# Reordering the start, the prologue and the paired output loop of a fused linear-attention and MLP kernel (forward and all gradients, one core)

## The chip, the core and the metric

The kernel runs on one core of a Trainium2 chip. The metric is the device time of one execution in microseconds (us). A profile is one execution taken by the hardware profiler; its "span" runs from the first to the last instruction and is 1.7 to 1.8 us shorter than the device time of the same execution.

Engines are named as in the profile: PE is TensorE's matmuls, PEld its weight loads, DVE is VectorE, ACT is ScalarE, POOL is GpSimd, and SP is the engine whose queue issues most of the DMAs here. "Releaser" means the last event that an instruction waited for.

## The reference

The inputs have a sequence of S = 2048 rows and width D = 640. The function is a gated mix of a linear attention and a ReLU MLP with F = 1728 hidden columns. The task is its output and the gradients with respect to six inputs.

```python
def _A_ref(x, wqkv, wo):                      # H = 32 heads of 20 columns
    q, k, v = split(x @ wqkv)
    phi = lambda t: jnp.where(t > 0, t + 1, jnp.exp(t)) + 1e-6
    pq, pk = phi(q), phi(k)
    kv = einsum("bhsd,bhse->bhde", pk, v)
    z  = einsum("bhsd->bhd", pk)
    o  = einsum("bhqd,bhde->bhqe", pq, kv) / (einsum("bhqd,bhd->bhq", pq, z)[..., None] + 1e-6)
    return o.reshape(B, S, D) @ wo
def _B_ref(x, w1, w2):
    return jnp.maximum(x @ w1, 0) @ w2
# ... shortened: the reshapes into heads and the types are left out
g = sigmoid((x * gate_w).sum(-1, keepdims=True))
out = g * _A_ref(x, wqkv, wo) + (1 - g) * _B_ref(x, w1, w2)
# outputs: out, and the gradients of A_x, A_wqkv, A_wo, B_w1, B_w2, gate_w for a given grad_out
```

## The kernel before

The sequence is cut into 16 chunks of 128 rows. The change touches the first third of the kernel, which goes like this on PE:

1. Start: some warm-up matmuls on a zeroed buffer, transposes of the first x chunks on PE (`xt`), and the k products (`k_chunk`), whose weights carry `gate_w` as a 641st column.
2. `yp`: five tiles of Y = pk' x. Each is transposed by a DMA on its way to `Y_s`.
3. Prologue ("the middle" below): h of chunks 0 and 1, a block-diagonal product `bd`, five tiles of `M`, each again transposed by a DMA, q and h of chunk 2.
4. Main loop: for each chunk, a q product, two halves of h (each 10 matmuls), and an output product `out_chunk`, which needs h of the chunk, and pq of the chunk, both transposed by DMAs.

h has 13.5 blocks of 128 columns. The last half block of two neighbouring chunks is handled by a **tail pair**: one chunk's half uses rows 0 to 63 of the array, the other's rows 64 to 127. So the tail pair of chunk i (even) needs the transposed h of chunk i **and** of chunk i+1.

All DMA transposes are issued from SP's queue, in its program order. This is the code that matters (cuts are marked):

```python
# helpers: L325 is the matmul in mm_cols (most products have this line)
def load_T(dst, src):
    return nc.sync.dma_start_transpose(dst, src.rearrange("s (c p) -> s c p", p=P))

# ---- start
x_load(0, 1)
nc.scalar.dma_start(wk_s[:, 0:2, 0:D], ...)           # two loads of wk
nc.scalar.dma_start(wk_s[:, 2:5, 0:D], ...)
nc.scalar.dma_start(wk_s[:, :, D:D + 1], gate_w.rearrange("(k p o) -> p k o", p=P, o=1))
x_load(1, 2)
x_load(2, G)
# ... cut
for n in range(9):
    nc.tensor.matmul(wp_[:, 0, :], lhsT=warm[:, 0:P], rhs=warm, start=True, stop=True)
# ... cut
xt(0)
xt(1)
for i in range(NT):
    if i + 2 < XPE * G:
        xt(i + 2)
    k_chunk(i)

# ---- q_post ends with   load_T(pqTs[i], pg)   once POOL has made pg
# ---- h_half(i, 1) ends with   load_T(hTs[i], hs(i))
def tail_pair(psA, psB, lA, lB, rhs, last):
    for b, (a, e) in enumerate(DSPL):
        nc.tensor.matmul(psA[:, b, 0:e - a], lhsT=lA[0:FT], rhs=rhs[0:FT, a:e], ...)    # L500
        nc.tensor.matmul(psB[:, b, 0:e - a], lhsT=lB[FT:P], rhs=rhs[FT:P, a:e], ...)    # L501

# ---- middle
h_half(0, 0)
# ... cut: zp, zb
q_den(0)
q_den(1)
h_half(0, 1)
blockdiag(KVT_s, wv_s, Y_s)
q_post(0)
h_half(1, 0)
for t in range(KD):
    mp = pp("mtp")
    win_mms(mp, lambda j: wo_s[:, j, csl(t)], KVT_s)
    copy_out(t, MT_s[:, t, :], flat(mp)[:, 0:D])
    load_T(M_s[:, :, csl(t)], MT_s[:, t, :])
q_post(1)
h_half(1, 1)
# ... cut: three DMAs
do_load(0)
# ---- main loop
LAG = 2
for i in range(2, NT + LAG):
    if i < NT and i % G == 1:
        do_load(i // G)
    if i < NT:
        q_main(i)
        q_den(i)
        h_half(i, 0)
        q_post(i)
        if i % 2 == 0 or i == NT - 1:
            h_half(i, 1)
    if i % 2 == 0 and i <= NT:
        q_store(i // 2 - 1)
    if i >= LAG:
        out_chunk(i - LAG)
    if i < NT - 1 and i % 2 == 1:
        h_half(i, 1)
# ---- loads of the next stage
for g in range(NG):
    load_T(doTg[g], do2[g * G * P:(g + 1) * G * P, :])
    if g < NSP:
        load_N(pqgg[g], pqg_d[g * G * P:(g + 1) * G * P, :])
```

## Time and profile before

| | before |
|---|---|
| device time, median of 4 runs | 646.46 us (645.88 to 647.41) |
| profiled execution | 646.82 us, span 645.0 us |
| PE busy | 636.6 us, 99% of the span |
| idle PE time between its first and last matmul | 4.2 us, of which 3.9 us in four gaps |
| from PE's last matmul to the end | 2.9 us |

The first two parts of the profile page that matter are the busy times (time, share of the span, instructions) and the engines' shares of the chain that ended last:

```profile
PE 636.6 (99%) x4458; PEld 355.3 (55%) x4458; DVE 240.3 (37%) x491; ACT 152.6 (24%) x224; POOL 97.8 (15%) x97
...
PE 94%; DMA 3%; ACT 1%; DVE 1%; issue 0%; POOL 0%; ACTq 0%; SPq 0%; DVEq 0%
```

PE works nearly all the time, so only idle PE time is to be had. The waits of PE name it (engine, product, line, releaser: total us, times, longest us):

```profile
PE op L501 <- DMA arena<-arena: 1.6, 2, 0.9
PE warm L385 <- DVE arena L372: 1.3, 1, 1.3
PE xtp L401 <- DMA arena<-in_A_x_dram: 1.2, 1, 1.2
PE bd L358 <- DMA arena<-arena: 1.1, 1, 1.1
```

The first entry is two tail pairs waiting for a transposed h. The timeline of PE shows where the waits are (start us, duration us, engine, line, operation, idle time before it in brackets). First the start:

```profile
5.07 1.27 PE L401 MATMUL xtp<-ident,arena 128*128 128x128 bf16 x10
7.56 0.45 PE L401 MATMUL xtp<-ident,arena 128*128 128x128 bf16 x5 [1.22 <-DMA arena<-in_A_x_dram]
7.85 1.69 PE L325 MATMUL kp<-arena 128*128 128x512 bf16 x10
```

The first k product begins at 7.85, after a third x chunk has been waited for. Then the middle and the first tail pair:

```profile
59.04 1.12 PE L358 MATMUL bd<-arena 128*128 128x140 bf16 x15
61.27 0.77 PE L358 MATMUL bd<-arena 128*128 128x140 bf16 x10 [1.11 <-DMA arena<-arena]
...
72.72 5.05 PE L325 MATMUL op<-arena 128*128 128x512 bf16 x36
77.71 0.39 PE L500 MATMUL op<-arena 64*128 64x512 bf16 x1
79.02 0.39 PE L501 MATMUL op<-arena 64*128 64x512 bf16 x1 [0.92 <-DMA arena<-arena]
...
79.39 0.93 PE L325 MATMUL qp<-arena 128*128 128x512 bf16 x5
```

`bd` stops after 15 matmuls for Y's last transposed tile. At 77.71 one half of the tail pair runs, and its partner only when the transposed h(1) has landed. The next product starts 1.69 us after the pair began.

### The profile page before, as it was taken

Reading aid. Unit: us, or ns where it says so; the run is one execution under the profiler, and the core shown is the slowest. Engines: PE = TensorE matmul, PEld = TensorE weight load, DVE = VectorE, ACT = ScalarE, POOL = GpSimd, SP = SyncE. Lnnn points to the kernel's source line nnn. Section 1 sums busy time; section 2 is a strip of 40 time slices with the busy share of each in tenths; the row PEclk is TensorE's granted clock in tenths of the full one; section 3 lists DMA queues with packets and bytes.
Section 4 is the critical chain, followed back from the end, with each engine's and each line's share of the span. In section 5 each row is a group of like instructions: output and inputs, shape, how many; then the busy total and the mean of one; then the engine's idle time right before and its main releaser. Section 6 shows DMA issues by size and latency. Waiting matters only on the chain.

```text
span 645.0 us, 10527 instructions
## 1 busy us (share of the span) xinstructions
PE 636.6 (99%) x4458; PEld 355.3 (55%) x4458; DVE 240.3 (37%) x491; ACT 152.6 (24%) x224; POOL 97.8 (15%) x97
## 2 busy tenths in 40 slices
PE   8999999999999999999999999999999999999998
PEld 4555555555555555555555555555555555555554
DVE  3823554454545135655145322130016320104442
ACT  3612222221222123232144343441100111110000
POOL 5002533434334013232001000000000000000000
PEclk9999999999999999999999999999999999999999
DMA  8999964253547953952979997692227549991111
GB/s 207 372 361 243 212 171 116 66 140 95 103 91 126 233 145 104 184 149 83 190 159 216 266 247 142 155 296 64 81 80 163 137 134 251 244 250 42 42 42 42
DMA packets 228409, 103.85 MB, mean 161 GB/s; under 512 B 185098, under 2 KB 227658, under 8 KB 228362
## 3 DMA queue, kind: packets, MB, share of 16 engines
q1 hardware_dynamic: 217050, 90.07, 59.4%
q10 hardware_dynamic: 11312, 13.11, 6.0%
q8 instruction: 35, 0.57, 0.4%
q14 instruction: 12, 0.10, 0.0%
HBM read 28.43 MB, written 28.84 MB: 89 GB/s over the span
## 4 chain that ended last, share of the span: by engine, by line
PE 94%; DMA 3%; ACT 1%; DVE 1%; issue 0%; POOL 0%; ACTq 0%; SPq 0%; DVEq 0%
PE op L325 11%; PE dxp L325 9%; PE gp L701 9%; PE w1p L787 9%; PE w2p L325 9%; PE dp L325 9%; PE hp L487 8%; PE qp L325 3%; PE kp L325 3%; PE yp L325 3%; PE rp L325 3%; PE wkp L325 3%; PE dkp L325 3%; PE xp L685 3%; PE wqp L874 3%; DMA arena<-arena 2%
## 5 line engine op out<-in xcount | busy, mean ns | idle before, releaser
L325 PEld LDWEIGHTS <-arena 128*128 128x128 bf16 x2818 | 218.0, 98 | 169.1 <-issue 2.4
L325 PE MATMUL op<-arena 128*128 128x512 bf16 x576 | 80.7, 299 | 0.0
L487 PE MATMUL hp<-arena 128*128 128x432 bf16 x320 | 62.3, 346 | 0.0
L325 PE MATMUL dxp<-arena 128*128 128x512 bf16 x450 | 61.5, 299 | 0.0
L701 PE MATMUL gp<-arena 128*128 128x432 bf16 x320 | 60.9, 346 | 0.1
L787 PE MATMUL w1p<-arena 128*128 128x432 bf16 x320 | 60.1, 346 | 0.0
L325 PE MATMUL dp<-arena 128*128 128x512 bf16 (+1 forms) x416 | 59.6, 299 | 0.0
L325 PE MATMUL w2p<-arena 128*128 128x512 bf16 (+1 forms) x416 | 59.3, 299 | 0.0
L787 PEld LDWEIGHTS <-arena 128*128 128x128 bf16 x320 | 30.8, 98 | 26.9 <-issue 0.5
L701 PEld LDWEIGHTS <-arena 128*128 128x128 bf16 x320 | 30.5, 98 | 27.0 <-issue 1.7
L487 PEld LDWEIGHTS <-arena 128*128 128x128 bf16 x320 | 30.3, 98 | 25.6
L708 DVE TENSOR_TENSOR arena<-tb,tb 128x864 bf16<-128x864 bf16 x32 | 19.4, 607 | 66.1 <-ACT tb L705 66.0
L456 POOL TENSOR_TENSOR f<-tb,zb 128x640 f32<-128x640 bf16 x16 | 23.3, 1459 | 111.4 <-DVE tb L369 57.8
L705 ACT ACTIVATE tb<-gp,omg_t 128x864 bf16<-128x864 f32 x32 | 31.4, 980 | 31.7 <-PE gp L701 28.4
L771 DVE TENSOR_TENSOR tb<-dkp,dzb 128x640 bf16<-128x640 f32 x16 | 13.1, 819 | 62.5 <-PE dkp L325 62.5
L522 DVE SCALAR_TENSOR_TENSOR tb<-op,arena 128x640 bf16<-128x640 f32 x16 | 13.2, 824 | 48.0 <-ACT arena L520 48.0
L520 ACT CAST arena<-op 128x640 bf16<-128x640 f32 x16 | 11.1, 692 | 83.1 <-PE op L500 43.5
L605 POOL TENSOR_TENSOR f<-zb,grd 128x640 f32<-128x640 bf16 x16 | 20.3, 1268 | 60.2 <-DVE grd L603 60.2
L896 DVE TENSOR_TENSOR arena<-dxp,f 128x640 bf16<-128x640 f32 x15 | 12.3, 823 | 37.0 <-PE dxp L325 37.0
L790 ACT CAST arena<-w1p 128x864 bf16<-128x864 f32 x10 | 8.8, 878 | 72.5 <-PE w1p L787 72.5
L325 PE MATMUL rp<-arena 128*128 128x512 bf16 (+1 forms) x160 | 24.3, 299 | 0.0
L325 PE MATMUL qp<-arena 128*128 128x512 bf16 (+1 forms) x160 | 24.2, 299 | 0.0
(125 smaller groups left out, 624.1 us busy)
## 6 DMA issues: line engine op xcount, KB each, us to landing
arena<-in_A_x_dram SPq DMA_DIRECT2D x7, 640.0 KB, 6.6
out_dram<-arena ACTq DMA_DIRECT2D x28, 160.0 KB, 3.2
pk_d<-arena SPq DMA_DIRECT2D x4, 640.0 KB, 9.3
arena<-in_grad_out_dram SPq DMA_DIRECT2D x4, 640.0 KB, 5.9
e_d<-arena SPq DMA_DIRECT2D x8, 320.0 KB, 3.6
out_dram<-arena ACTq DMA_DIRECT2D x8, 320.0 KB, 2.7
arena<-e_d SPq DMA_DIRECT2D x8, 320.0 KB, 3.5
dq_d<-arena SPq DMA_DIRECT2D x8, 320.0 KB, 4.0
```

What stands on the lines that cost most here:

```text
L325: mm = nc.tensor.matmul(ps_tile[:, b, 0:e - a], lhsT=lhsT, rhs=rhs_fn(a, e), start=start, stop=stop, **kw)
L456: nc.gpsimd.tensor_tensor(tzs[i][:], pqs[i][:], zb[:], ALU.mult)
L487: nc.tensor.matmul(hp[:, nb, 0:NBW], lhsT=xT(i, k), rhs=w1_s[:, k, blk * NBW:(blk + 1) * NBW], start=(k == 0), stop=(k == KD - 1))
L522: nc.vector.scalar_tensor_tensor(jk[:], flat(op)[:, 0:D], 1.0, doX(i)[:, 0:D], ALU.mult, ALU.mult, accum_out=T_t[:, i:i + 1])
L605: nc.gpsimd.tensor_tensor(heads(wz[:]), heads(zb[:]), hb(w32[:]), ALU.mult)
L685: nc.tensor.matmul(xp[:, 0, :], lhsT=lhsT, rhs=doX(i)[:, 0:512], start=(i == 0), stop=(i == NT - 1))
L701: nc.tensor.matmul(gp[:, nb, 0:NBW], lhsT=doTg[i // G][:, k, gsl(i)], rhs=w2T_s[:, k, blk * NBW:(blk + 1) * NBW], start=(k == 0), stop=(k ...
L705: nc.scalar.activation(gs[:], gp[:, :, 0:NBW], ACT.Copy, scale=omg_t[:, i:i + 1])
L708: nc.vector.tensor_tensor(hs(i)[:, rng], msk[:], gs[:].rearrange("p b c -> p (b c)"), ALU.mult)
L771: nc.vector.tensor_tensor(a_[:], flat(kp)[:, 0:D], dzb[:], ALU.add)
L787: nc.tensor.matmul(wp[:, nb, 0:NBW], lhsT=xN2[:, i, csl(m)], rhs=hs(i)[:, blk * NBW:(blk + 1) * NBW], start=(i == 0), stop=(i == NT - 1))
L874: nc.tensor.matmul(wp[:, 0, :], lhsT=lhsT, rhs=dqN[:, i, 0:512], start=(i == 0), stop=(i == NT - 1))
```

## The change

The intent is to remove each of these waits by order alone:

- **Start.** wk comes in five loads; `gate_w` comes as five contiguous rows and is transposed on PE; only x chunk 0 is transposed before the first k product; 8 warm-ups instead of 9.
- **Middle.** Both halves of h(1) are moved forward, one ahead of `bd` and one ahead of the M tiles; q(2) and half of h(2) go between and into the M tiles. M's five DMA transposes become one of 25 blocks, behind all five tiles (`M_s` gets another layout for it).
- **Main loop.** Chunks are handled in pairs: q(a), h(a), q(a+1) and the first half of h(a+1) come ahead of out(a-2).
- **End of the loop.** The loads of grad_out and pq for the next stage are ordered behind the last transpose of h (`after`).

The diff, cut to its core:

```diff
+    M_s = aview("M", KD * D).rearrange("p (t c s) -> p t c s", t=KD, c=KD)
+    def after(late, early):        # order of two DMAs on their queue, no semaphore
+        tc.add_manual_dep(late.ins, early.ins.name, ...)
...
+    wk_load(nc.scalar, 0)
     x_load(0, 1)
-    nc.scalar.dma_start(wk_s[:, 0:2, 0:D], ...)
-    nc.scalar.dma_start(wk_s[:, 2:5, 0:D], ...)
-    nc.scalar.dma_start(wk_s[:, :, D:D + 1], gate_w.rearrange("(k p o) -> p k o", p=P, o=1))
+    wk_load(nc.scalar, 1)
+    wk_load(nc.sync, 2)
+    wk_load(nc.scalar, 3)
+    wk_load(nc.sync, 4)
+    nc.scalar.dma_start(gst[:], gate_w.rearrange("(k p) -> k p", p=P))
...
-    for n in range(9):
+    for n in range(NWARM):          # 8
...
     xt(0)
-    xt(1)
+    nc.tensor.transpose(tp[:, 0, 0:KD], gst[:], ident[0:KD, 0:KD])
+    nc.scalar.copy(wk_s[:, :, D:D + 1], tp[:, 0, 0:KD].unsqueeze(2))
     for i in range(NT):
+        k_chunk(i)
+        if i == 0:
+            xt(1)
         if i + 2 < XPE * G:
             xt(i + 2)
-        k_chunk(i)
...
     q_den(0)
-    q_den(1)
     h_half(0, 1)
+    h_half(1, 0)
+    q_post(0)
     blockdiag(KVT_s, wv_s, Y_s)
-    q_post(0)
-    h_half(1, 0)
-    # loop over five M tiles, each with its own load_T; q_post(1); h_half(1, 1)
+    h_half(1, 1)
+    q_main(2)
+    mt_tile(0)
+    mt_tile(1)
+    mt_tile(2)
+    h_half(2, 0)
+    mt_tile(3)
+    mt_tile(4)
+    M_ld = nc.sync.dma_start_transpose(M_s..., MT_s...)       # 25 blocks
+    q_den(1)
+    q_post(1)
+    q_den(2)
...
-    for i in range(2, NT + LAG):
-        # the loop shown above
+    for a in range(2, NT + LAG, 2):
+        if a < NT:
+            if a % G == 2 and a // G + 1 < NG:
+                do_load(a // G + 1)
+            if a > 2:
+                q_main(a)
+                q_den(a)
+                h_half(a, 0)
+            q_post(a)
+            h_half(a, 1)
+            q_main(a + 1)
+            q_den(a + 1)
+            h_half(a + 1, 0)
+            q_post(a + 1)
+        q_store(a // 2 - 1)
+        out_chunk(a - 2)
+        if a < NT:
+            h_half(a + 1, 1)
+        out_chunk(a - 1)
...
     for g in range(NG):
-        load_T(doTg[g], do2[g * G * P:(g + 1) * G * P, :])
+        after(load_T(doTg[g], do2[g * G * P:(g + 1) * G * P, :]), hT_ld[0])
         if g < NSP:
-            load_N(pqgg[g], pqg_d[g * G * P:(g + 1) * G * P, :])
+            after(load_N(pqgg[g], pqg_d[g * G * P:(g + 1) * G * P, :]), hT_ld[0])
```

(`hT_ld[0]` is the last `load_T(hTs[i], hs(i))`. Three stores in the middle are also put behind `M_ld` with `after`.)

More of the change, by code (lines that the diff above doesn't have):

```diff
@@ L225 @@
     pkN = aview("pk", NT * D, i=NT)
-    Y_s, YT_s, KVT_s, M_s, MT_s = mat("Y"), mat("YT"), mat("KVT"), mat("M"), mat("MT")
+    Y_s, YT_s, KVT_s, MT_s = mat("Y"), mat("YT"), mat("KVT"), mat("MT")
+    M_s = aview("M", KD * D).rearrange("p (t c s) -> p t c s", t=KD, c=KD)
     dwoT_s, dwo_s = mat("dwoT"), mat("dwo")
@@ L315, in load_T @@
         return nc.sync.dma_start_transpose(dst, src.rearrange("s (c p) -> s c p", p=P))
+    def after(late, early):
+        tc.add_manual_dep(late.ins, early.ins.name, mybir.DependencyInfo(
+            mybir.DependencyClass.NoSync, mybir.DependencyReason.DATA), reason="order of loads")
     def load_N(dst, src):
-        nc.sync.dma_start(dst, src.rearrange("(i p) d -> p i d", p=P))
+        return nc.sync.dma_start(dst, src.rearrange("(i p) d -> p i d", p=P))
     def rows2(t, pr):
@@ L374, in x_load, with wk_load @@
         load_N(xN[:, a:b, 0:D], x2[a * P:b * P, :])
+    def wk_load(eng, k):
+        eng.dma_start(wk_s[:, k, 0:D], A_wqkv[k * P:(k + 1) * P, D:2 * D])
+    wk_load(nc.scalar, 0)
     x_load(0, 1)
-    nc.scalar.dma_start(wk_s[:, 0:2, 0:D], A_wqkv[0:2 * P, D:2 * D].rearrange("(k p) j -> p k j", p=P))
-    nc.scalar.dma_start(wk_s[:, 2:5, 0:D], A_wqkv[2 * P:5 * P, D:2 * D].rearrange("(k p) j -> p k j", p=P))
-    nc.scalar.dma_start(wk_s[:, :, D:D + 1], gate_w.rearrange("(k p o) -> p k o", p=P, o=1))
+    wk_load(nc.scalar, 1)
[3 more added lines that the diff above has]
+    nc.scalar.dma_start(gst[:], gate_w.rearrange("(k p) -> k p", p=P))
     x_load(1, 2)
@@ L382 @@
     nc.gpsimd.memset(xN[:, :, D:D + 1], 1.0)
+    NWARM = 8
     wp_ = pp("warm")
-    for n in range(9):
+    for n in range(NWARM):
         nc.tensor.matmul(wp_[:, 0, :], lhsT=warm[:, 0:P], rhs=warm, start=True, stop=True)
@@ L416 @@
     xt(0)
-    xt(1)
+    tp = psp.tile([P, KD, P], BF16, tag="PP", bufs=4, name="gwtp")
+    nc.tensor.transpose(tp[:, 0, 0:KD], gst[:], ident[0:KD, 0:KD])
+    nc.scalar.copy(wk_s[:, :, D:D + 1], tp[:, 0, 0:KD].unsqueeze(2))
     for i in range(NT):
+        k_chunk(i)
+        if i == 0:
+            xt(1)
         if i + 2 < XPE * G:
             xt(i + 2)
-        k_chunk(i)
         if i == 0:
@@ L478, in q_store @@
         if pr in pq_st:
-            nc.sync.dma_start(rows2(pqg_d, pr), pq_st.pop(pr))
-        nc.sync.dma_start(rows2(e_d, pr), e_st.pop(pr))
+            st_ = nc.sync.dma_start(rows2(pqg_d, pr), pq_st.pop(pr))
+            if pr == 0:
+                after(st_, M_ld)
+        st_ = nc.sync.dma_start(rows2(e_d, pr), e_st.pop(pr))
+        if pr == 0:
+            after(st_, M_ld)
+    hT_ld = [None]
     def h_half(i, half):
@@ L495, in h_half @@
             hTs[i] = rnext("hTf").rearrange("p (c s) -> p c s", s=P)
-            load_T(hTs[i], hs(i))
+            hT_ld[0] = load_T(hTs[i], hs(i))
     def tail_pair(psA, psB, lA, lB, rhs, last):
@@ L513, in out_chunk @@
         for k in range(KD):
-            mm_cols(op, pqT[:, k, :], lambda a, e: M_s[:, k, a:e], False, ii == 1 and k == KD - 1)
+            mm_cols(op, pqT[:, k, :], lambda a, e: M_s[:, a // P:e // P, k, :], False, ii == 1 and k == KD - 1)
         if ii == 0:
@@ L551, with mt_tile @@
     q_den(0)
-    q_den(1)
     h_half(0, 1)
+    h_half(1, 0)
+    q_post(0)
     blockdiag(KVT_s, wv_s, Y_s)
-    q_post(0)
-    h_half(1, 0)
-    for t in range(KD):
+    h_half(1, 1)
+    def mt_tile(t):
         mp = pp("mtp")
@@ L560 @@
         copy_out(t, MT_s[:, t, :], flat(mp)[:, 0:D])
-        load_T(M_s[:, :, csl(t)], MT_s[:, t, :])
+    q_main(2)
[5 more added lines that the diff above has]
+    mt_tile(4)
+    M_ld = nc.sync.dma_start_transpose(M_s.rearrange("p t c s -> p (t c) s"),
+                                       MT_s.rearrange("e t (c p) -> e (t c) p", p=P))
+    q_den(1)
     q_post(1)
-    h_half(1, 1)
-    nc.sync.dma_start(KVT_d.rearrange("(k p) d -> p k d", p=P), KVT_s)
+    q_den(2)
+    after(nc.sync.dma_start(KVT_d.rearrange("(k p) d -> p k d", p=P), KVT_s), M_ld)
     nc.sync.dma_start(YT_d.rearrange("(k p) d -> p k d", p=P), YT0_s)
@@ L568 @@
     LAG = 2
-    for i in range(2, NT + LAG):
-        if i < NT and i % G == 1:
-            do_load(i // G)
-        if i < NT:
-            q_main(i)
-            q_den(i)
-            h_half(i, 0)
-            q_post(i)
-            if i % 2 == 0 or i == NT - 1:
-                h_half(i, 1)
-        if i % 2 == 0 and i <= NT:
-            q_store(i // 2 - 1)
-        if i >= LAG:
-            out_chunk(i - LAG)
-        if i < NT - 1 and i % 2 == 1:
-            h_half(i, 1)
+    for a in range(2, NT + LAG, 2):
[17 more added lines that the diff above has]
+        out_chunk(a - 1)
     e_r, dq_st = {}, {}
@@ L670 @@
                 ld = load_T(w2T_s[:, :, q_ * 432:(q_ + 1) * 432], B_w2[q_ * 432:(q_ + 1) * 432, :])
-                tc.add_manual_dep(ld.ins, last_mm.ins.name, mybir.DependencyInfo(
-                    mybir.DependencyClass.NoSync, mybir.DependencyReason.DATA), reason="loads of dw2 first")
+                after(ld, last_mm)
     r_store(NT // 2 - 1)
```

## The prediction

> What bounds the kernel. The page's engine table gives PE 636.6 us busy of a 645.0 us span (99%), granted clock 1.00; the chain of waits is 94% PE. The change removes one warm-up matmul, adds one small transpose and keeps the rest of PE's work, so it can only win idle PE time. The PE timeline and PE waits list that: 1.3 us before the first warm-up matmul, 1.2 us (6.3 to 7.6) for x chunks 2 and 3, 1.1 us in the block-diagonal product (60.2 to 61.3) for the last transposed Y tile, 0.9 us (78.1 to 79.0) and 0.7 us (about 217) in tail pairs of the output product for a transposed h, 2.9 us at the end. Of 8.4 us, some 5 (0.8%) are in play: the end is untouched.
>
> Start. Before, three x chunks are transposed ahead of the first k product at 7.85. The gate column, loaded as 2-byte elements, lands 6.4 us after issue, and DMA falls from 370 to about 40 GB/s at 6.5 to 7.2. The Trainium skill ("DMA: Bandwidth & Descriptors", rules for kernel authors) says a non-contiguous last dimension becomes one descriptor per element; the dip agrees. After, gate_w comes as five rows and a PE transpose, wk in five loads. From bytes and landings of before I estimate gate row and x chunk 1 landing at 6.0 to 6.4: PE waits some 0.7 us after x0's transpose, first k matmul near 6.1, but chunks 1 to 3 are transposed later than before. Net gain 0.5 us. Risk: at 6.0 PE is slow (107 ns per 128-column transpose, 56 ns at 7.6). "TensorE: Matmul & The Clock Gate" (part 1) puts warm-up at one busy, free-running window of about 3.4 us; another idle gap could move it.
>
> Middle. One more h half (1.83 us) precedes the block-diagonal product, so Y's last tile (landed 61.2) is in time: 1.1 us gained. h(1)'s second half comes before the M tiles and its transpose ahead of M's, instead of behind five M transposes (1.2 us of issue each on the SP queue): the 0.9 us goes. M's five transposes become one of 25 blocks, estimated 5 us to landing (2.4 us for 5 blocks, 3.4 for 14); from the last M tile to M's first use PE has 8.5 us of work, so no new wait, 2 to 3 us slack. A new wait of 0.3 us is possible: h(2) needs a PSUM tile.
>
> Main loop. Pairing reorders work; PE is 10.00 of 10 there and stays so: zero gain.
>
> End of the loop. Loads of grad_out for the next stage are held behind the last h transpose: the 0.7 us goes; the first r product, 12 us later, has them in time.
>
> Sum: 0.5 + 1.1 + 0.9 + 0.7 - 0.3 = 2.9 us. Prediction 643.5 us, range 642.0 to 645.4. Faster by over 2%: 0.01; within 2%: 0.98; slower by over 2%: 0.01.
>
> What would show it: PE waits lose the block-diagonal, both tail-pair and the x entries; PE busy stays 636 to 637; first k product near 6.1; no wait for M; loop at 10.00 of 10; end still 2.9.
>
> What would make it wrong: chunk 0's k product at the slow clock (up to 1.4 us lost); M's transpose late behind other DMAs, or DVE late with the block-diagonal mask or the M tiles (1 to 3 us before out(0)); x chunks 2, 3 late, since their load now waits for an earlier load's semaphore.

## The result, and the profile after

| | before | changed |
|---|---|---|
| device time, median | 646.15 us (16 runs, 645.51 to 648.07) | 642.38 us (10 runs, 642.16 to 643.89) |
| profiled execution | 646.82 us, span 645.0 | 642.35 us, span 640.6 |
| PE busy | 636.6 us | 635.2 us |
| ratio | | 0.994, 95% interval 0.993 to 0.9951 |

Ratios here are the mean time of one kernel's fast runs over that of the other's fast runs of the same rounds, so they are not quite the ratio of the medians. The change is within 2%, a gain of 3.8 us by the medians.

The same two parts of the page of the changed kernel:

```profile
PE 635.2 (99%) x4458; PEld 354.5 (55%) x4458; DVE 241.2 (38%) x491; ACT 152.7 (24%) x225; POOL 98.6 (15%) x97
...
PE 98%; DMA 1%; ACT 1%; issue 0%; SPq 0%; DVE 0%
```

The chain is now 98% PE. The waits of PE (the helper lines moved: L330 is the old L325, L509 the old L487, L352 the old L347, L363 the old L358):

```profile
PE warm L397 <- DVE arena L377: 1.3, 1, 1.3
PE gwtp L430 <- DMA gst<-in_gate_w_dram: 0.4, 1, 0.4
PE hp L509 <- ACT arena L335: 0.3, 1, 0.3
PE xtp L413 <- DMA arena<-in_A_x_dram: 0.3, 1, 0.3
```

The `bd` wait and both tail-pair waits are gone. At the start, a short wait for the gate rows is new, and the one for x has shrunk from 1.22 to 0.29 us. In the middle one of 0.31 us is new: h(2) waits until ACT (L335) has copied an M tile out of PSUM. The timeline of the start:

```profile
4.64 0.74 PE L413 MATMUL xtp<-ident,arena 128*128 128x128 bf16 x5
5.77 0.17 PE L430 MATMUL gwtp<-ident,gst 5*128 5x5 bf16 x1 [0.39 <-DMA gst<-in_gate_w_dram]
5.97 0.39 PE L330 MATMUL kp<-arena 128*128 128x512 bf16 x1
6.64 0.45 PE L413 MATMUL xtp<-ident,arena 128*128 128x128 bf16 x5 [0.29 <-DMA arena<-in_A_x_dram]
```

The first k matmul is at 5.97 instead of 7.85. Its chunk's other nine follow at 6.93, because the scheduler put the five transposes of x chunk 1 in between. And the middle with the first tail pair:

```profile
60.02 1.73 PE L363 MATMUL bd<-arena 128*128 128x140 bf16 x25
...
66.31 1.99 PE L509 MATMUL hp<-arena 128*128 128x432 bf16 x10 [0.31 <-ACT arena L335]
...
73.85 5.05 PE L330 MATMUL op<-arena 128*128 128x512 bf16 x36
78.83 0.39 PE L522 MATMUL op<-arena 64*128 64x512 bf16 x1
78.83 0.39 PE L523 MATMUL op<-arena 64*128 64x512 bf16 x1
...
79.21 0.36 PE L509 MATMUL hp<-arena 128*128 128x432 bf16 x1
```

`bd` runs its 25 matmuls without a stop. The two halves of the tail pair now start at the same time, 78.83, and the next product follows 0.38 us later. So a pair that runs side by side costs 0.38 us, and the disturbed one of before cost 1.69 us: 1.31 us were lost, not the 0.92 us of the bracket. The Trainium skill ("TensorE: Matmul & The Clock Gate", Part 3) says that matmuls on different rows of the array run at the same time; this trace agrees, with one start for both halves.

To see where the 4.37 us of span went, I cut both profiles at products that both have: the first q product, the first matmul of h(0), the first output matmul, the last output matmul, the first product of dw1, and the end. In the paired order, q(3) and the first half of h(3) come before the first output product. They take 1.36 + 1.83 = 3.19 us of PE, which I take out of the middle and put into the loop, so that both kernels do the same work in each part.

| part | before | changed | difference |
|---|---|---|---|
| start to first q product | 30.09 | 29.25 | -0.84 |
| Y tiles (q products to h(0)) | 25.03 | 25.03 | 0.00 |
| middle (h(0) to first output product) | 17.60 | 19.57 - 3.19 = 16.38 | -1.22 |
| loop (first to last output matmul) | 149.49 | 143.97 + 3.19 = 147.16 | -2.33 |
| last output matmul to the first dw1 product | 215.54 | 215.45 | -0.09 |
| first dw1 product to PE's last matmul | 204.37 | 204.37 | 0.00 |
| from PE's last matmul to the end | 2.89 | 2.99 | +0.10 |

The loop's 2.33 us are the two tail pairs: 1.31 us for the first and 1.02 us for the last (it took 1.40 us where the changed kernel's takes 0.38).

Two cautions about the sizes. First, the profiled execution of before, at 646.82 us, is itself about 0.9 us above the most common runs of its kernel, so the table overstates the typical gain by that much. Much of this may be the last tail pair. The profile of e1 (below: the kernel before with the new start) has no wait there, and five of e1's six runs, with a mean of 644.85 us, lie 0.96 us under the eight common runs of before of the same rounds (mean 645.81), about what the new start alone explains. So the common run of before probably loses only the first pair's 1.31 us in the loop; no profile of such a run shows it. Second, the runs of before form two groups. Over the 44 runs of before made beside the experiments, 24 lie at 645.3 to 646.4 us, all with a mean granted clock of 1.00; 20 lie at 647.0 to 648.4, and 14 of these have a clock of 0.997. The changed kernel had 0.997 in none of 11 runs. I return to this below.

### The profile page after: what moved, and what is told of

It reads as the page before. It is cut to its first block, busy times and chain, and to the rows that moved or that the text cites. A ratio compares the mean times of both kernels' runs of the same rounds, so it can differ in the third digit from the quotient of the medians.

```text
span 640.6 us, 10514 instructions
## 1 busy us (share of the span) xinstructions
PE 635.2 (99%) x4458; PEld 354.5 (55%) x4458; DVE 241.2 (38%) x491; ACT 152.7 (24%) x225; POOL 98.6 (15%) x97
## 4 chain that ended last, share of the span: by engine, by line
PE 98%; DMA 1%; ACT 1%; issue 0%; SPq 0%; DVE 0%
PE op L330 12%; PE dxp L330 10%; PE hp L509 9%; PE gp L736 9%; PE w1p L822 9%; PE w2p L330 9%; PE dp L330 9%; PE yp L330 3%; PE qp L330 3%; PE rp L330 3%; PE wkp L330 3%; PE dkp L330 3%; PE kp L330 3%; PE xp L720 3%; PE wqp L909 3%; PE xp L721 1%
## 5 line engine op out<-in xcount | busy, mean ns | idle before, releaser
L330 PEld LDWEIGHTS <-arena 128*128 128x128 bf16 x2818 | 218.3, 98 | 168.0 <-issue 0.3
L330 PE MATMUL op<-arena 128*128 128x512 bf16 x576 | 80.7, 299 | 0.0
L509 PE MATMUL hp<-arena 128*128 128x432 bf16 x320 | 62.6, 346 | 0.3 <-ACT arena L335 0.3
L330 PE MATMUL dxp<-arena 128*128 128x512 bf16 x450 | 61.5, 299 | 0.0
L330 PE MATMUL dp<-arena 128*128 128x512 bf16 (+1 forms) x416 | 59.6, 299 | 0.0
L330 PE MATMUL w2p<-arena 128*128 128x512 bf16 (+1 forms) x416 | 59.3, 299 | 0.0
L509 PEld LDWEIGHTS <-arena 128*128 128x128 bf16 x320 | 30.0, 98 | 26.9 <-issue 2.3
L330 PE MATMUL rp<-arena 128*128 128x512 bf16 (+1 forms) x160 | 24.4, 299 | 0.0
L330 PE MATMUL qp<-arena 128*128 128x512 bf16 (+1 forms) x160 | 24.2, 299 | 0.0
```

The source lines that it names most:

```text
L330: mm = nc.tensor.matmul(ps_tile[:, b, 0:e - a], lhsT=lhsT, rhs=rhs_fn(a, e), start=start, stop=stop, **kw)
L509: nc.tensor.matmul(hp[:, nb, 0:NBW], lhsT=xT(i, k), rhs=w1_s[:, k, blk * NBW:(blk + 1) * NBW], start=(k == 0), stop=(k == KD - 1))
```

## The experiments

The account in the prediction is: each edit removes the wait that it is aimed at, and pairing the loop adds nothing. The rival that the trace of after suggested is: in the middle another chain stands right behind the wait for Y, and in the loop it is pairing, together with the held loads, that decides when the last pieces of h are transposed, because they stand in one in-order queue with other transposes. Each expectation below names its own theories: A is the account tested, B its rival. All twelve kernels gave correct results. The traces of these runs lack about 80 of the 4458 matmul records, which does not change the marks used here.

| run | what it is | median (before of the same rounds) | ratio, 95% | runs at clock 0.997 or below |
|---|---|---|---|---|
| e1_start | before + new start | 644.88 (645.99) | 0.9981 [0.9965, 0.9997] | 0 of 6 |
| e2_bd | before + h(1) first half ahead of bd | 648.45 (645.99) | 1.0029 [1.0012, 1.0047] | 3 of 6 |
| e3_h1 | before + h(1) second half ahead of M | 647.59 (645.99) | 1.0035 [1.0004, 1.0065] | 3 of 6 |
| e4_end | before + held loads | 646.82 (645.99) | 1.0011 [0.9993, 1.0029] | 0 of 6 |
| f2_pairhold | before + pairing + held loads | 644.73 (646.23) | 0.9981 [0.9963, 0.9998] | 2 of 6 |
| e5_fiveM | changed, five M transposes | 642.72 (647.57) | 0.9929 [0.9916, 0.9942] | 0 of 5 |
| e6_unpaired | changed, loop not paired | 646.05 (647.57) | 0.998 [0.9967, 0.9993] | 0 of 5 |
| e7_gatecol | changed, old load of the gate column | 643.96 (647.57) | 0.9948 [0.9933, 0.9963] | 0 of 5 |
| e8_warm1 | changed, one warm-up matmul | 643.69 (646.23) | 0.9954 [0.994, 0.9969] | 0 of 5 |
| e9_nohold | changed, loads not held | 647.88 (647.57) | 1.0012 [0.9994, 1.0029] | 5 of 6 |
| f1_cand | changed, other start, PSUM wait removed | 645.76 (646.23) | 0.9986 [0.9965, 1.0007] | 4 of 6 |
| g1_psum | changed, PSUM wait removed | 642.22 (646.37) | 0.9939 [0.9924, 0.9954] | 0 of 6 |

The before kernel's median differs between rounds (645.99 to 647.57) because its two groups are drawn in different shares. So differences of less than 2 us between runs of different rounds are not read from the ratios here but from the parts of the traces:

| part, us | before | e1 | e2 | e3 | e4 | f2 | changed | e5 | e6 | e9 | g1 |
|---|---|---|---|---|---|---|---|---|---|---|---|
| start to first q product | 30.09 | 29.01 | 29.97 | 29.90 | 30.39 | 30.10 | 29.25 | 29.61 | 29.01 | 29.21 | 29.02 |
| middle | 17.60 | 17.60 | 17.99 | 17.06 | 17.61 | 17.61 | 16.38 | 16.38 | 16.38 | 16.38 | 16.07 |
| loop | 149.49 | 148.51 | 149.34 | 149.97 | 149.74 | 147.17 | 147.16 | 147.41 | 150.21 | 153.64 | 147.17 |

(The 3.19 us of the paired order are taken out of the middle and put into the loop, as before.)

### e1: the start alone

```diff
# before, plus the start part of the change (five wk loads, gate rows and their
# transpose, k_chunk ahead of xt, 8 warm-ups); nothing else
```

> The kernel before, with the start alone changed (gate as five rows and a PE transpose, wk in five loads, k product of chunk 0 ahead of the transposes of chunks 1 to 3, 8 warm-ups). Theory A (the start's gain is carried through): all marks of PE from the third k chunk on are 0.84 us earlier than before, also after the block-diagonal product, and the span ends 0.8 us earlier. Rival B (the last transposed Y tile is bound by the DMA queue, not by PE): its landing stays at 61.2, the wait in the block-diagonal product grows from 1.1 to about 1.9 us and nothing of the 0.84 is left at the end. The waits in the two tail pairs (0.9 and 0.6 us) stay in both.

Measured: the first q product is 1.08 us earlier than in the profile of before, and the first output product also 1.08 us. The waits in the middle and loop:

```profile
PE op L511 <- DMA arena<-arena: 1.0, 1, 1.0
PE bd L358 <- DMA arena<-arena: 0.5, 1, 0.5
PE hp L497 <- DVE arena L332: 0.5, 1, 0.5
```

The start is worth about 0.9 us: the mean of the first q product over five profiles with the old start is 30.09 us, and over six with the new one 29.18 us, each with a scatter of about 0.3 us. The prediction had 0.5.

The middle is the lesson of this run. The wait for Y fell from 1.11 to 0.51 us, but the middle still takes 17.60 us, because h(1)'s second half now waits 0.46 us for DVE (L332), which copies an M tile. DVE reaches the M tiles through a reduction for q, a ReLU and the mask of `bd`, and this chain ends 9.63 us after the start of the `zp` product in both profiles. So the wait for Y had a second limit hidden right behind it. f2, e4 and e1 all show 17.60 or 17.61 with different splits of the wait.

### e2 and e3: one half of h(1) moved forward, alone

```diff
# e2, against before
     h_half(0, 1)
+    h_half(1, 0)
     blockdiag(KVT_s, wv_s, Y_s)
     q_post(0)
-    h_half(1, 0)
```

> The kernel before, with the first half of h(1) moved ahead of the block-diagonal product and nothing else. Theory A (the wait for the last Y tile just goes): no wait in the block-diagonal product, PE 1.26 us earlier from there on. Rival B (the h half had covered the masking on DVE, 1.2 us in five pieces, between the block-diagonal product and the M tiles): the wait moves to the M tiles, 1.0 to 1.5 us there, and the gain at the first output product is under 0.3 us.

```diff
# e3, against before
     h_half(1, 0)
+    h_half(1, 1)
     for t in range(KD):
         # five M tiles with their transposes
     q_post(1)
-    h_half(1, 1)
```

> The kernel before, with the second half of h(1) moved ahead of the M tiles and nothing else. Theory A (the first tail pair waited for h(1)'s transpose because it was queued behind M's transposes): h(1)'s transpose is issued 3 or more us earlier, the wait of 0.92 us in the first tail pair goes, and from there on PE is 1.31 us earlier (the pair took 1.69 us from its first matmul to the next product where it takes 0.38 undisturbed). Rival B (the DMA queue is full of other things there, and what is put later becomes the new last): M's last transposes land later and the output product waits for M instead, gain under 0.4 us.

Neither run gained: both ratios are above 1, and middle and loop together take 0.24 us more than in before in e2 and 0.06 us less in e3, although neither profile has the wait in the last tail pair. The waits of e2:

```profile
PE mtp L347 <- DVE arena L362: 1.5, 1, 1.5
...
PE op L325 <- DMA arena<-arena: 0.9, 1, 0.9
...
```

e2 has no `bd` wait, but with nothing left between `bd` and the M tiles, these wait 1.49 us for DVE's mask (L362). Its middle is longer than before's by 0.39 us, and the M tiles' transposes come late for the first output product (0.86 us). e3 in turn has no first tail wait, because h(1) is transposed earlier. But its transpose stands in SP's queue ahead of M's, and the output product waits for M:

```profile
PE op L325 <- issue: 1.6, 1, 1.6
...
PE op L325 <- DMA arena<-arena: 0.9, 1, 0.9
```

"issue" here means that the profile shows no event for this wait. I put it to M as well, because SP's queue in e3 shows eight transposes in a row from 64.91 to 77.33 us, with M's last ones among them, and the wait falls on the first matmul that needs M (77.26).

So neither move of h(1), alone, gives what the prediction booked for it. Each only exchanges the wait for another.

### e4 and f2: the held loads alone, and pairing with held loads

```diff
# e4, against before
-    load_T(doTg[g], do2[g * G * P:(g + 1) * G * P, :])
+    after(load_T(doTg[g], do2[g * G * P:(g + 1) * G * P, :]), hT_ld[0])
     if g < NSP:
-        load_N(pqgg[g], pqg_d[g * G * P:(g + 1) * G * P, :])
+        after(load_N(pqgg[g], pqg_d[g * G * P:(g + 1) * G * P, :]), hT_ld[0])
```

> The kernel before, with the loads of grad_out and of the stored q tiles held behind the last h transpose and nothing else. Theory A: the wait of 0.64 us in the last tail pair goes, PE is 1.02 us earlier from there on, no new wait in the next stage, span 1.0 us shorter. Rival B (pairing of the loop or the earlier issue did it, not the order of loads): the wait stays, span unchanged. Rival C: the r products of the next stage wait for grad_out, gain lost.

```diff
# f2, against before: e4's edit, and the paired loop
-    for i in range(2, NT + LAG): ...
+    for a in range(2, NT + LAG, 2): ...        # as in the change, q and h of chunk 2 inside
```

> The kernel before, with the paired loop and the held loads and nothing else (start, block-diagonal order, five M transposes as before). Theory A (pairing with the held loads removes both tail-pair waits by itself, as 3.2 us more PE work comes ahead of the first output product and the last h transpose is issued early): the wait of about 1.1 us in the block-diagonal product stays, no wait in any tail pair, PE 2.3 us earlier at the end of the loop, median some 2 us under the kernel before. Rival B (the reordered prologue is needed for the first tail pair): its wait stays at 0.5 us or more, gain at most 1.0 us.

The held loads alone leave both tail waits in place. The last one is the same 0.64 us as in before:

```profile
217.54 0.39 PE L507 MATMUL op<-arena 64*128 64x512 bf16 x1 [0.64 <-DMA arena<-arena]
```

Pairing with held loads removes both. Its first tail pair:

```profile
80.91 0.39 PE L506 MATMUL op<-arena 64*128 64x512 bf16 x1
80.91 0.39 PE L507 MATMUL op<-arena 64*128 64x512 bf16 x1
```

The two halves of its last pair start together too, at 214.68. f2's loop takes 147.17 us, like the changed kernel's 147.16, with the old start and the old middle. Its waits in the middle are still those of before, split anew: 0.74 us for Y and 0.24 us for DVE's copy of an M tile.

So in the profiles the loop's whole 2.33 us come from pairing with the held loads, not from the move of h(1) and not from holding the loads as such. By the runs it is less: the four of f2's six that had the full clock lie 1.40 us under the eight common runs of before of the same rounds (means 644.62 and 646.02), close to the first pair's 1.31 us. Pairing without held loads was tried only on the changed kernel (e9).

SP's queue shows how, for the last pair. In before:

```profile
206.10 3.57 SPq L315 DMA_TRANSPOSE arena<-in_grad_out_dram  x1
209.78 2.86 SPq L315 DMA_TRANSPOSE arena<-arena  x2
```

PE ends h(15) at about 206.1 us. In the queue ahead of its transpose stand one of grad_out (3.57 us of issue) and the transpose of pq(15), which waits for POOL. The last h transpose is the second of the pair at 209.78; it is issued at 211.10, 5.0 us after PE's part. In e4 the grad_out transpose is out of the way:

```profile
209.82 1.20 SPq L315 DMA_TRANSPOSE arena<-arena  x1
211.11 0.53 SPq L484 DMA_DIRECT2D e_d<-arena  x1
211.75 1.66 SPq L315 DMA_TRANSPOSE arena<-arena  x1
```

Yet h's is issued only at 211.75: pq(15)'s is ahead of it as before, and so now is a store, which in before went behind it. Counted from the start of PE's last matmul of h(15), pq(15) is issued after 3.87 us in before and 3.36 us in e4, so holding the load did free 0.5 us; but h is issued after 5.19 and 5.29 us, because the store took that time. In e1, e2 and e3, where grad_out keeps the queue for only 2.5 to 2.8 us and no store comes between, h is issued after 4.66 us and the last pair doesn't wait. In the changed kernel:

```profile
204.41 1.52 SPq L316 DMA_TRANSPOSE arena<-arena  x1
206.03 4.05 SPq L316 DMA_TRANSPOSE arena<-in_grad_out_dram  x1
```

PE ends h(15) at about 202.7 and its transpose is issued at 204.41. In the paired order pq(15) is made ahead of out(12) and h(15)'s second half behind it, so the transpose of pq(15) has left the queue by then. It lands at 209.76 and is used at 212.60: 2.8 us to spare. For the first pair, pairing puts 3.19 us of other PE work ahead of out(0), more than the 1.31 us by which h(1) was late.

### e5: five transposes of M instead of one

```diff
# against the changed kernel
     def mt_tile(t):
         ...
+        return load_T(M_s[:, t, :, :], MT_s[:, t, :])
...
-    mt_tile(4)
-    M_ld = nc.sync.dma_start_transpose(M_s..., MT_s...)     # 25 blocks
+    M_ld = mt_tile(4)
```

> The changed kernel, with M's one transpose of 25 blocks put back into five of 5 blocks, each issued when its M tile is copied. Theory A (issue time on the SP queue is what the middle runs out of: five took 1.2 to 1.9 us each, one takes 3.2): M's last piece lands at about 77.5 to 79, PE waits 0.5 to 1.5 us for it before the M part of the first output product (needed at 77.4), the span grows by as much. Rival B (only the order of h(1) against M mattered, the single transpose is for looks): no wait for M, span within 0.2 us of the changed kernel's 640.6.

Its middle is the same 16.38 us, but M is waited for. The idle time is only 0.08 us; yet the first matmul that needs M comes 3.78 us after the chunk's first, where it is 3.53 us in the changed kernel, so 0.25 us are lost, and the loop takes 147.41 us. The span is 641.0 against 640.6 us: 0.36 us of it is at the start, which this edit does not touch, 0.25 us is this wait, and the end is 0.28 us shorter. The result lies between theories A and B. The single transpose is worth 0.25 us here and is not what the gain rests on: with 3.19 us more PE work ahead of out(0), five transposes are almost in time.

### e6: the changed kernel without pairing

```diff
-    for a in range(2, NT + LAG, 2): ...
+    for i in range(2, NT + LAG):        # the loop of before; q and first half of h only if i > 2
```

> The changed kernel, with the main loop back to one chunk a step (start, middle, one M transpose and held loads kept). Theory A (pairing gets the last h transpose past the q transpose of the same chunk, which waits for POOL in the same SP queue): the last h transpose is issued some 5 us after its h half, as before, instead of 1.7; it lands within about 0.3 us of its use, so a wait of 0 to 0.65 us in the last tail pair (0 to 1.0 us of span). Rival B (holding the next stage's loads removed that wait, the prediction's reading): no wait, span as the changed kernel's 640.6. Under A and B alike, PE stays at 10.00 of 10 within the loop.

```profile
PE op L330 <- DMA arena<-arena: 1.8, 1, 1.8
PE op L523 <- DMA arena<-arena: 0.7, 1, 0.7
```

Taking the pairing away costs 3.05 us in the loop (150.21 against 147.16 us). The 1.75 us of the first line is M's single transpose, now late by itself; the second is the last tail pair. Its h transpose stood behind the transpose of pq(15) and a store and was issued at 209.50, though nothing of grad_out was ahead of it. So the new prologue with one transpose of M depends on pairing: the edits do not add up one by one.

### e9: the changed kernel without held loads

```diff
-    after(load_T(doTg[g], ...), hT_ld[0])
+    load_T(doTg[g], ...)
     if g < NSP:
-        after(load_N(pqgg[g], ...), hT_ld[0])
+        load_N(pqgg[g], ...)
```

> The changed kernel, with the next stage's loads no longer held behind the last h transpose. Theory A (pairing gives the slack): no wait in the last tail pair, span within 0.2 us of 640.6; one grad_out transpose is issued ahead of the last h transpose but its 3 to 4 us fit in the slack of 10 us. Rival B (the prediction's: the order of those loads was the cause): a wait of 0.6 us or more comes back, span up by about 1.0 us.

The loop takes 6.48 us longer: theory A is refuted, and the loss is far above the 1.0 us of B. The wait and the queue:

```profile
PE op L523 <- DMA arena<-arena: 3.1, 1, 3.1
```

```profile
206.62 4.16 SPq L316 DMA_TRANSPOSE arena<-in_grad_out_dram  x1
210.89 1.61 SPq L316 DMA_TRANSPOSE arena<-arena  x1
```

In the paired order the grad_out transpose can go earlier than the last h transpose, so the hold, worth nothing alone, is needed. Half of the loss is of another kind. These are stretches of time (window, its length, busy time of PE, PEld, DVE, ACT and POOL with instructions, granted PE clock, DMA share, GB/s):

```profile
213.00:216.00 3.00, 0.00 (x0) 0.00 (x0) 0.00 (x0) 0.00 (x0) 0.00 (x0) 0.91 1.09 214
216.00:219.00 3.00, 2.95 (x12) 1.28 (x13) 0.83 (x2) 0.69 (x1) 0.00 (x0) 0.50 1.12 241
219.00:222.00 3.00, 3.00 (x13) 1.37 (x11) 0.00 (x0) 0.00 (x0) 0.00 (x0) 0.50 1.30 166
222.00:226.00 4.00, 3.95 (x30) 2.27 (x30) 0.76 (x2) 0.69 (x1) 0.72 (x1) 0.97 0.66 167
```

PE stood idle for 3.11 us and then ran at half its clock for about 6 us, which costs about 3 us more. The Trainium skill ("TensorE: Matmul & The Clock Gate", Part 1) says that the clock falls back after an idle window of about 3.4 us, and that this window runs freely. This trace agrees roughly: the wait is 3.11 us, a little shorter than that figure. Five of e9's six runs had a clock of 0.995 or 0.997; the sixth, with 1.0, was the fastest, at 646.57 us.

### e7 and e8: the start taken apart

```diff
# e7, against the changed kernel
-    nc.scalar.dma_start(gst[:], gate_w.rearrange("(k p) -> k p", p=P))
+    nc.scalar.dma_start(wk_s[:, :, D:D + 1], gate_w.rearrange("(k p o) -> p k o", p=P, o=1))
-    # transpose of gst on PE, and its copy
```

> The changed kernel, with the gate column loaded again as 2-byte elements, no PE transpose for it; wk in five loads and the order of the start kept. Theory A (the 640 elements of 2 bytes hold up the DMA engines behind them): the column lands at 7 to 8, DMA falls to some 40 GB/s for about 1 us, x chunks 2 and 3 or the column itself are waited for, and PE is 0.5 to 1.2 us later from the third k chunk on than in the changed kernel. Rival B (the start's gain is the order of work alone): less than 0.3 us later.

```diff
# e8, against the changed kernel
-    NWARM = 8
+    NWARM = 1
```

> The changed kernel, with 1 warm-up matmul instead of 8. Theory A (warm-ups buy the full clock by about 6.5 us): x0 is transposed from about 4.0 on its landing and the first k matmul starts at 5.3 to 5.6, but PE stays at half clock (107 ns a 128-column transpose) until 8.5 to 11, and from the third k chunk on PE is 1 to 3 us later than in the changed kernel. Rival B (the clock does not depend on them, PE waits for data anyway): third k chunk within 0.3 us of 10.2 or earlier.

In e7 the first k product waits for the gate column. This is the rest of that product:

```profile
7.20 2.41 PE L330 MATMUL kp<-arena 128*128 128x129 bf16 x9 [0.62 <-DMA arena<-in_gate_w_dram]
```

The nine matmuls take 2.41 us. In the changed kernel they take 1.31 us from 6.93 on. So this profile loses twice: by its waits, and by PE at half speed until about 10.3 us. That the waits prolong the slow stretch isn't shown: g1 waits 0.81 us at the same place, and its next matmul, at 6.26, takes the full-speed 0.39 us. The third k chunk begins 2.46 us later than in the changed kernel. This profile is the slowest of e7's five runs; by the medians e7 loses 1.6 us (643.96 against 642.38, in different rounds). The Trainium skill ("DMA: Bandwidth & Descriptors", rules for kernel authors) says that a load with a non-contiguous last dimension becomes one descriptor per element; the runs show what this does here: in before the column's 1.2 KB took 6.36 us from issue to landing, and in e7 4.95 us. The five contiguous rows of the changed kernel are used 3.56 us after their issue.

In e8 the first k matmul comes at 5.87 us, no later than with eight warm-ups. But:

```profile
6.80 2.46 PE L330 MATMUL kp<-arena 128*128 128x129 bf16 x9
```

Chunk 0's nine matmuls take 2.46 us where they took 1.31, and the third k chunk begins 1.51 us later. The seven other warm-ups cost nothing here, because the first k product waits for the gate rows in any case (their transpose is at 5.76 in e8 and 5.77 in the changed kernel), and are worth 1.5 us.

### f1 and g1: trying for more

```diff
# g1, against the changed kernel
     mt_tile(1)
-    mt_tile(2)
     h_half(2, 0)
+    mt_tile(2)
     mt_tile(3)
# f1: g1's edit; x_load(1, 2) ahead of wk's third load; wk 3 and 4 in one load behind
# the gate rows; xt(1) right behind xt(0)
```

> A candidate to beat the changed kernel: x chunk 1 loaded ahead of wk 2, gate row ahead of wk 3 and 4, these two in one load (8 loads in all, so that the load of x chunks 2 and 3 waits for no semaphore), chunk 1 transposed right after chunk 0; and h(2)'s first half after two M tiles instead of three. If the waits of the changed kernel are what it says: the waits for the gate row (0.4), for x chunk 1 (0.3) and for the PSUM tile (0.3) go, third k chunk 0.3 to 0.6 us earlier than 10.2, first output product 0.6 to 0.9 us earlier than 73.85, span 639.7 to 640.1. If the start is bound by the bytes instead: wk 3 and 4 land later than 6.4 and the gain is the 0.3 us of the PSUM wait alone.

> The changed kernel, with h(2)'s first half after two M tiles instead of three and nothing else, as the candidate to beat it. Theory: the one wait of PE that the change brought (0.31 us, for a PSUM tile whose copy stands behind an exponential on ACT) goes, as it went in the run before; from the first output product on PE is 0.3 us earlier than in the changed kernel where the starts are alike, span near 640.3, median 0.2 to 0.4 us under the changed kernel's. Rival: M's transpose then comes later and PE waits for M, no gain.

f1 failed at the start. The scheduler put x chunk 2's transposes ahead of the rest of the first k product, and these wait 1.32 us for a load that lands at 7.85 us. Its third k chunk begins 1.76 us later than the changed kernel's. g1 keeps only the swap in the middle. The wait for PSUM is gone and the middle takes 16.07 instead of 16.38 us, 0.31 us less. Its ratio of 0.9939 [0.9924, 0.9954] can't be told from the changed kernel's 0.994, and both were measured in different rounds; its profile, with a span of 640.2 us, is the shortest. It is the best version that I have, by the trace and not by the ratio.

## Why the prediction was right or wrong

The total was right: 642.38 us lies in the range of 642.0 to 645.4, and the class (within 2%) was given 0.98. But it lies near the lower end: the gain was 3.8 us where 2.9 were forecast. Several steps were wrong, and that the total fits is in part luck (see below).

**Right.** PE bounds the kernel, and only idle PE time could be won: PE busy went from 636.6 to 635.2, just below the 636 to 637 foreseen, and the chain of waits from 94 to 98% PE. The first k matmul was foreseen near 6.1 and came at 5.97. The `bd` wait and both tail waits vanished. M's single transpose was estimated at 5 us to landing and took 4.81 (issued 71.18, landed 75.99); it was in time, though by 1.4 us rather than 2 to 3. The possible new wait for PSUM was there, with 0.31 us. The end hardly changed (2.89 and 2.99 us). Of the entries that were to vanish, the one for x stayed, with 0.29 us.

**Mis-sized: the start.** "Net gain 0.5 us" was 0.84 us in the two profiles and 0.91 us as a mean of several profiles. The prediction named the risk that PE is slow at 6.0. It did not come true: transposes were slow until 5.07 at least, but by the profile the first k matmul, at 5.97, took 0.39 us, as at full speed, where it took 0.61 us in e7 and f1. The wait after x0's transpose was 0.39 us, not 0.7.

**Mis-sized: the tail pairs.** "The 0.9 us goes" and "the 0.7 us goes" were 1.31 and 1.02 us. The trace books as idle only the time in which nothing of PE ran. But while one half waits, the other half runs alone for 0.39 us in time that both would share. The gap has to be taken from the pair's start to the next product.

**Wrong: "Pairing reorders work; PE is 10.00 of 10 there and stays so: zero gain".** This is the main failed step. Pairing with held loads on the kernel before gives the whole 2.33 us of the loop in the profiles (f2), and the changed kernel without pairing loses 3.05 us there (e6). PE's work does not change in a full loop, but at its two ends pairing sets how long h's transposes have and what stands ahead of them in SP's queue.

**Wrong: what gains the first tail wait.** The prediction gave the 0.9 us to h(1)'s second half coming ahead of the M tiles. The cause was read rightly, since that move alone does remove the wait, but it pays with 1.58 + 0.90 us for M (e3). With pairing the wait goes even where h(1) is not moved (f2).

**Wrong: "Loads of grad_out for the next stage are held behind the last h transpose: the 0.7 us goes".** Held loads alone leave 0.64 us (e4): they free 0.5 us in SP's queue, and a store takes it. They are needed only beside pairing, where leaving them out costs 6.5 us (e9).

**Incomplete: the middle.** "One more h half (1.83 us) precedes the block-diagonal product, so Y's last tile (landed 61.2) is in time: 1.1 us gained" took Y's landing as the only bound. DVE's chain ended at nearly the same time (e1), and h(1)'s move alone made the middle longer (e2). The middle gained 1.22 us only because the new order hides both, with both halves of h(1) and q(2); this is argued from e1 and e2, since the pieces of the new order were not tried one by one. e6 shows that the middle gains as much without pairing. Against the forecast of 1.1 - 0.3 this was somewhat more.

Why the total fits all the same: the waits were read correctly, each was counted once, and the whole change did remove the `bd` and tail waits. Only what removed them was put down to the wrong edits: pairing gave 2.33 us in the profiles where 0 was forecast, and the two edits that were to give 0.9 and 0.7 us gave nothing by themselves. The sizes did not cancel: start, middle and loop gained 0.84 + 1.22 + 2.33 = 4.39 us in the profiles, where 0.5 + 0.8 + 1.6 = 2.9 were forecast. The measured gain of 3.8 us is nearer to the forecast, probably because the common runs of before lack the last tail wait; if so, this was luck. A reader who had kept just the edits that the prediction paid for, and left out pairing, would have had e6: about 646 us.

**Open.** 14 of 44 runs of before had a mean clock of 0.997, with a median of 647.88 us against 645.96 us for the 24 lower ones. A loss of 0.3% of 645 us is about 1.9 us, which fits about 4 us at half the clock. In kernels with the old start (before, e2, e3, e4, f2) this came in 22 of 68 runs, in those with the new start in none of 33 (changed kernel, e1, e5, e6, g1), leaving out e9, whose long wait explains it, and f1, whose start is another (4 of 6, with a wait of 1.32 us there). The profiles of before, e2, e3, f2 and f1 all have one wait of 1.2 to 1.6 us for x behind the warm-ups; e4, with no such run in 6, has two shorter ones (0.8 and 0.7 us), and e7 and e8 had none in 5 each. So it may be that the old start now and then loses the full clock again soon after it is granted. This is a correlation: no profile caught a run of before in that condition, and I have no experiment that sets only this. Six more runs of before, and two of the changed kernel at 643.8 to 643.9, lie 1.1 to 1.7 us above the others of their kernel at a clock of 0.999 to 1.00; they are not explained. Nor is it settled why the transpose of grad_out keeps SP's queue for 3.57 us in the profile of before and for 2.5 to 2.8 us in e1, e2 and e3, nor why the last h transpose lands between 5.1 and 5.9 us after its issue. The last tail wait of before hangs on both.

## What to carry to other kernels

When PE is full, list the idle gaps, and for each ask what stands second: remove the first cause alone and see whether the same time comes back under another name, as in e1, e2 and e3. An in-order queue of transposes is a shared resource; whatever waits in it for an engine (here pq for POOL) holds everything behind it, so an order of work that gives such transposes time can matter where the busy engine's total is unchanged. And when two pieces normally run side by side, measure a wait from the start of the pair to the next product, not by the idle time alone.

## What the Trainium skill lacked or had wrong

- "DMA: Bandwidth & Descriptors", section "Issuing engines are not separate DMA queues", says that the time to initiate a DMA is usually small relative to the DMA. For DMA transposes here it is not: the 25-block transpose of M kept SP's queue for 3.24 us and landed 4.81 us after its issue; the last transpose of h takes 1.5 us of the queue and lands after 5.4 us, one of grad_out takes 4.05 us of the queue (all in the changed kernel). Beside cycles per instruction for "previous generations" in its trn3 part, that page gives no queue time for a transpose, and I found none elsewhere; the order in this queue decided 2.33 us of the profiles.
- "DMA: Bandwidth & Descriptors", rules for kernel authors, gives one descriptor per element for a non-contiguous last dimension, but no time for it: 1.2 KB took 6.36 us to land in before and 4.95 us in e7, where the third k chunk came 2.46 us later than in the changed kernel (1.6 us by the medians).
- "TensorE: Matmul & The Clock Gate", Part 1, gives an idle window of about 3.4 us for the fall of the clock. Here a wait of 3.11 us was enough, with some 6 us at half the clock after it. That is under Part 1's figure, but fits the page's own table "Why this matters for your kernels", which warns of gaps over about 3 us; so the page gives two figures, and the second is the safer one. What lowers the mean clock to 0.997 in 14 of 44 runs of before stays open here: the longest wait after the first matmul in its profile is 1.22 us (that profile had a clock of 1.00).
- The same page warns (Part 1) that clock events in a trace have been seen to be unreliable, but does not name this case: the granted clock in the records at the start reads 1.00 from the first microsecond in these profiles, while five transposes take 0.74 us at 4.64 and 0.45 us at 6.64. The matmuls' durations, and not the granted clock, show when PE is at full speed.
